# A written order table, loads in smaller pieces, 64x64 transposes, filler matmuls and merged last stores in an attention and channel-mix kernel

## The chip, the cores and the metric

The kernel runs on one core of one Trainium2 chip. The metric is the device time of one execution in microseconds (us). Before the change three runs gave 204.72, 204.80 and 205.69, a median of 204.8.

## What is computed

Inputs are q, k and v, each of 8 batches x 8 heads x 576 positions x 64, two vectors mu_k and mu_r of 512, and three weights: w_k (512x1024), w_v (1024x512) and w_r (512x512). All are float32, and so is the output, 8 x 576 x 512.

```python
q_s = softmax(q over the 64 of a head);  k_s = softmax(k over the 576 positions)
kv  = einsum('bhsd,bhse->bhde', k_s, v);  x = einsum('bhsd,bhde->bhse', q_s, kv)  # heads side by side: 512
x_prev = x one position later, zero at position 0
xk = mu_k*x + (1-mu_k)*x_prev;  xr = mu_r*x + (1-mu_r)*x_prev
k = relu(xk @ w_k);  v = k*k @ w_v;  r = sigmoid(xr @ w_r);  out = r*v
```

The attention has no product of positions by positions: each head makes a 64x64 matrix kv, and q_s is multiplied by it. The channel mix that follows is three dense products over 4608 rows.

## The kernel before

**Attention.** The work goes by (batch b, group g of four heads), 16 pairs in all. A tile holds two heads on its 128 partitions, 64 partitions each with nine positions in a row, and two further heads beside them (index u). The names that the profile shows are these. Loads bring q, k and v as float32 into `raw` buffers, of which there are eleven. Loads of batch 0 (L257) go out on the queues of SP and ACT, those of v of batch 0 (L275) and all later ones on POOL's queue, those of batch 1 in two halves each. ACT takes exponentials of q and k into `eq` and `ek` (L383) and casts v into `vv` (L389). DVE sums q's exponentials, takes reciprocals and scales (L398, L402, L407) into `qs`, all bfloat16.

TensorE (PE) then does three things for the pair. T transposes q: 18 instructions of 64 partitions x 128 columns (L417). KV multiplies exp(k) with v: 36 products of 64x64 (L444), where v has a 65th column of ones that gives the sum Z of exp(k). For batch 0 v has no such column, and 36 more products with a vector of ones make Z (L441). DVE takes 1/Z (`rz`, L451) and scales kv with it (L461); ACT copies the transposed q from PSUM to `qt` (L424). X is the product of the two.

For batches 0 and 1 (`FUSED`) the weights of X already hold mu: DVE multiplies kv with mu and with 1 - mu into `wp` (L538, named wp with batch, group and m), and PE makes xk (m = 0) and xr (m = 1) directly, from q and from q one position earlier (L550); ACT and DVE each copy a half out (L560). For the other batches PE makes x (L591), ACT copies it out, and DVE forms the difference, scales it by mu and adds (L605 to L619). For these the X of one pair, T of the next and KV of the next are one piece of PE work, named B with batch and group in the texts below (TKV where it has no X, and X alone for the last pair). xk and xr stand in SBUF for four batches at a time.

**Channel mix.** 4608 columns are cut into ten units (`UNITS`: 512, 512, 512, 512 and 256 columns, twice). A unit has K, for each of eight 128-row pieces of w_k four matmuls of 128x512 (L687), followed by a relu on ACT (L672) and a square on DVE (L676); then for each tile of 128 rows R, four matmuls with w_r (L719) and a tanh on ACT (L724, which with the +1 in the next step is twice the sigmoid; the relu carries a factor for the half); and V, eight matmuls with w_v (L739), in two halves. DVE multiplies (tanh + 1) with V out of PSUM into one of five `ot` buffers (L745), and two stores of 64 rows of 2 KB each send the tile out (L757). The last tile is worked in two halves of its 512 columns, which gives four stores of 64 rows of 1 KB. Stores go out on SP's queue, the second of each pair of the last tile on ACT's.

**mu.** The two vectors are loaded as two rows (L283). PE spreads them over 128 partitions with one wide matmul and turns them into columns with four small ones (L315, L318); ACT and DVE copy them to SBUF (L324, L328, L330).

**Weights.** w_k comes in two loads of 1 MB (`wk_a`, `wk_b`), w_r in one, w_v in two (`wv_a`, `wv_b`), cast to bfloat16 on the way, on POOL's queue. All loads but the first ones are tied to the sixth load of batch 0 (`GATE`, L338 to L346).

**Order.** No loop over stages sets the order. A list scheduler (`Plan.order`, L158) has a cost for each piece of work, a due time, buffers as resources, and a rule by which PE counts twice when it had little to do lately (`warm`, L124). It picks what can start first and, among equals, what is due first. Each engine then runs its pieces in that order. PSUM has four banks for K, R and V (`mm`) and two pairs of banks for the attention (`att`); for batch 0 and the X of batch 0 either kind is taken (`any`).

Of the kernel before, what the change touches and what calls it, by code (L numbers as in the profile page):

```python
# [26 lines left out]
         "kvn": 2, "wp": 2, "xb": 2, "xd": 2, "xm": 3, "k2": 2, "rel": 3, "th": 2, "ot": 5,  # L27
         "mm": 4, "att": 2, "any": 4}
SHARED = {("any", 0): [("att", 0)], ("any", 1): [("att", 1)],
          ("any", 2): [("mm", 0), ("mm", 1)], ("any", 3): [("mm", 2), ("mm", 3)]}  # L30
KVO = 296
XO = 368

START = 0.7
HOP = 0.05
LATE = 1e6
LOOK = {"PE": 0.03, "ACT": 0.2, "DVE": 0.1, "POOL": 0.03, "SP": 0.03}
MAIN = 5.676
PACE = 1.116
DMA_LEAD = 2.0  # L40
DMA_TAIL = 0.6
LOAD_RATE = 375.0
CAST_RATE = 375.0
GATE = 5
FUSED = (0, 1)
ROWS = 1.05
MU_EARLY = 3.0
BLOCK_LOOK = 0.4
EARLY_UNITS = 2
AHEAD = {(0, 0): 0, (0, 1): 0.64, (1, 0): 3.95, (1, 1): 5.45, (2, 0): 10.46, (2, 1): 5.14, (3,  # L50
        0): 9.42, (3, 1): 7.74, (4, 0): 0, (4, 1): 10.55, (5, 0): 2.05, (5, 1): 11.13, (6, 0):
        16.45, (6, 1): 16.13, (7, 0): 1.76, (7, 1): 3.64}
FIRST = ((0, 0, ("SP", "SP")), (0, 1, ("SP", "SP")), (1, 0, ("SP", "ACT")), (1, 1, ("SP",
        "SP")))
SOON = {(1, 0, 0): 4.53, (1, 0, 1): 4.87}
PASSES = 3


class Slot:

    def __init__(self, pool):
        self.pool = pool
        self.index = None
        self.rank = self.since = None
        self.last = []


class Op:

    def __init__(self, engine, occ, lat, key, emit, deps, takes, gives, size, rate, name):  # L70
        self.engine, self.occ, self.lat, self.key = engine, occ, lat, key
        self.emit, self.deps, self.takes = emit, list(deps), list(takes)
        self.size, self.rate, self.name = size, rate, name
        self.start = self.end = self.made = None
        self.early = 0.0
        self.main = False
        self.look = 0.0
        for slot in gives:
            slot.last.append(self)


class Plan:

    def __init__(self):
        self.pools = {name: [SHARED.get((name, i), [(name, i)]) for i in range(n)]
                      for name, n in POOLS.items()}
        self.ops = []

    def add(self, engine, occ, lat, key, emit, deps=(), takes=(), gives=(), size=0.0, rate=1.0,
            name=""):  # L90
        op = Op(engine, occ, lat, key, emit, [d for d in deps if d is not None], takes, gives,
                size, rate, name)
        self.ops.append(op)
        return op

    def places(self, op):
        t, got = 0.0, []
        for slot in op.takes:
            if slot.index is not None:
                t = max(t, slot.since)  # L100
                continue
            best = None
            if slot.rank is not None and slot.rank != self.next.get(slot.pool, 0):
                return None
            for i, parts in enumerate(self.pools[slot.pool]):
                if (slot.pool, i) in got:
                    continue
                free = 0.0
                for part in parts:
                    user = self.user.get(part)  # L110
                    if user is not None:
                        if not user.last or any(o.end is None for o in user.last):
                            free = None
                            break
                        free = max(free, max(o.end for o in user.last) + HOP)
                if free is not None and (best is None or free < best[0]):
                    best = (free, i)
            if best is None:
                return None
            t = max(t, best[0])  # L120
            got.append((slot.pool, best[1]))
        return t, got

    def warm(self, t):  # L124
        busy = 0.0
        for s, e in reversed(self.pe_busy):
            if e < t - 3.4:
                break
            busy += min(e, t) - max(s, t - 3.4)
        return busy > 2.0  # L130

    def set_due(self):
        for op in self.ops:
            op.due = op.key
        for op in reversed(self.sorted):
            if not op.size and not op.main:
                for o in self.after[op]:
                    op.due = min(op.due, o.due - op.lat - HOP)
                op.due -= op.early

    def prepare(self):
        self.after = {op: [] for op in self.ops}
        for op in self.ops:
            for d in op.deps:
                self.after[d].append(op)
        left = {op: len(op.deps) for op in self.ops}
        ready = [op for op in self.ops if not op.deps]
        self.sorted = []
        while ready:
            op = ready.pop()  # L150
            self.sorted.append(op)
            for o in self.after[op]:
                left[o] -= 1
                if not left[o]:
                    ready.append(o)
        assert len(self.sorted) == len(self.ops)

    def order(self):  # L158
        self.set_due()
        self.user = {}  # L160
        self.next = {}
        self.pe_busy = []
        dma_free = 0.0
        out = {"HW": [], "SW": []}
        free, able, done = {}, {}, []
        left = {}
        for op in self.ops:
            op.start = op.end = None
            for slot in op.takes:
                slot.index = None  # L170
            left[op] = len(op.deps)
            able.setdefault(op.engine, [])
            if not op.deps:
                able[op.engine].append(op)
        n = len(self.ops)
        while len(done) < n:
            chosen = None
            for engine, ops in able.items():
                now = free.get(engine, START)
                ready = None  # L180
                for op in ops:
                    t = now
                    for d in op.deps:
                        t = max(t, d.end + HOP)
                    if op.size:
                        ends = out["SW" if op.engine == "POOL" else "HW"]
                        if len(ends) >= 8:
                            t = max(t, ends[-8] + 0.3)
                    if op.takes:
                        found = self.places(op)  # L190
                        if found is None:
                            continue
                        t = max(t, found[0])
# [8 lines left out]
            for slot, (_, i) in zip(fresh, self.places(op)[1] if fresh else ()):  # L202
                slot.since = t
                slot.index = i
                if slot.rank is not None:
                    self.next[slot.pool] = slot.rank + 1
# [704 lines left out]
```

## Time and profile before

| what | value |
|---|---|
| median of three runs | 204.8 us |
| the profiled execution | 205.87 us, of which the span of the profile is 204.1 |
| PE busy | 187.9 us, 92%, 1930 records |
| weight loads of PE | 93.9 us, 46% (they lie beside matmuls) |
| DVE busy | 152.7 us, 75% |
| ACT busy | 146.8 us, 72% |
| POOL busy | 38.6 us, 19% |
| DMA | 16431 packets, 40.10 MB, mean 197 GB/s |
| the chain that ended last | PE 78%, DMA 13%, DVE 3%, ACT 2% |

The span is what the profiler saw of the program, and the rest of the execution's time lies around it. Busy shares are means over the whole span, so a stage in which one engine waits and a stage in which it never stops are mixed in them; the windows of the prediction take them apart. In a row of a timeline the columns are: start (us), length, engine, line, operation, what is written and what is read, the shape, the count, and in brackets the idle time of the engine just before, with what ended it.

### The profile page before, as it was taken

The page shows a single profiled execution, that of the slowest core. Times are in us where ns is not written, and L with a number is a line of the kernel's source. Part 1 is how long each engine was busy: PE and PEld are TensorE (multiplying, and loading weights), DVE is VectorE, ACT ScalarE, POOL GpSimd, SP SyncE. Part 2 cuts the span into 40 slices and gives each one's busy share as a digit, 9 for nine tenths or more (in the row PEclk, how much of TensorE's full clock was granted, in tenths as well). Part 3 has the DMA queues.
Part 4 walks back from the last instruction along what each step waited for, and adds up shares of the span by engine and source line. Part 5 has one row for each costly group of instructions (what it writes and reads, how often), then busy time and mean ns, then how long its engine had stood idle before and what let it go on. Part 6 is the DMA issues. An engine that isn't in the chain of part 4 may idle for free.

```text
span 204.1 us, 4851 instructions
## 1 busy us (share of the span) xinstructions
PE 187.9 (92%) x1930; PEld 93.9 (46%) x1930; DVE 152.7 (75%) x348; ACT 146.8 (72%) x226; POOL 38.6 (19%) x61
## 2 busy tenths in 40 slices
PE   0659999979999999999999999999999999999990
PEld 0445444534454444444466444444444444444750
DVE  1865478999889989999999995999825459622620
ACT  4463689999999999999999488777624752642520
POOL 4912269433223312532000000000000000000000
PEclk9999999999999999999999999999999999999997
DMA  6999999999999994999742220422044012404303
GB/s 206 277 247 206 256 404 391 399 405 405 392 393 400 410 385 137 368 348 401 224 102 53 48 58 3 100 57 53 0 100 110 0 41 65 103 0 103 90 16 104
DMA packets 16431, 40.10 MB, mean 197 GB/s; under 512 B 2196, under 2 KB 5528, under 8 KB 16408
## 3 DMA queue, kind: packets, MB, share of 16 engines
q0 software_dynamic: 9328, 27.99, 41.6%
q1 hardware_dynamic: 6696, 11.25, 19.7%
q10 hardware_dynamic: 384, 0.56, 0.8%
q8 instruction: 15, 0.25, 0.5%
q14 instruction: 8, 0.07, 0.1%
HBM read 33.56 MB, written 9.44 MB: 211 GB/s over the span
## 4 chain that ended last, share of the span: by engine, by line
PE 78%; DMA 13%; DVE 3%; ACT 2%; POOL 1%; issue 0%; DVEq 0%; ACTq 0%
PE mm_b L739 9%; PE mm_c L739 9%; PE mm_d L739 7%; PE mm_b L687 7%; DMA wr<-in_moe_w_r_dram 7%; PE mm_c L687 7%; PE mm_d L687 7%; PE mm_a L687 7%; PE mm_a L719 6%; DMA raw_g<-in_v_dram 4%; PE mm_a L739 4%; PE mm_d L719 3%; PE mm_c L719 3%; PE mm_b L719 3%; DMA raw_b<-in_q_dram 2%; PE att_b L444 1%
## 5 line engine op out<-in xcount | busy, mean ns | idle before, releaser
L687 PEld LDWEIGHTS <-wk_a 128*128 128x128 bf16 x160 | 15.3, 99 | 17.0 <-issue 1.8
L687 PEld LDWEIGHTS <-wk_b 128*128 128x128 bf16 x160 | 15.5, 98 | 15.3 <-issue 0.2
L719 PEld LDWEIGHTS <-xr 128*128 128x128 bf16 x144 | 13.9, 98 | 16.8 <-ACT xr L563 0.9
L739 PEld LDWEIGHTS <-k_a 128*128 128x128 bf16 x144 | 13.8, 98 | 16.4
L739 PEld LDWEIGHTS <-k_b 128*128 128x128 bf16 x152 | 14.2, 98 | 14.7 <-issue 0.2
L719 PE MATMUL mm_a<-wr,xr 128*128 128x512 bf16 x56 | 14.4, 379 | 0.4 <-DMA raw_g<-in_v_dram 0.4
L724 ACT ACTIVATE th_a<-mm_a 128x512 f32<-128x512 f32 x14 | 8.4, 602 | 7.2 <-PE mm_a L719 7.1
L687 PE MATMUL mm_b<-xk,wk_a 128*128 128x512 bf16 (+1 forms) x44 | 11.2, 371 | 0.0
L687 PE MATMUL mm_c<-xk,wk_a 128*128 128x512 bf16 (+1 forms) x40 | 10.2, 371 | 0.0
L687 PE MATMUL mm_a<-xk,wk_a 128*128 128x512 bf16 (+1 forms) x40 | 9.8, 360 | 0.3 <-DVE xk L560 0.3
L687 PE MATMUL mm_c<-xk,wk_b 128*128 128x512 bf16 (+1 forms) x40 | 9.4, 358 | 0.0
L687 PE MATMUL mm_d<-xk,wk_b 128*128 128x512 bf16 (+1 forms) x40 | 9.4, 358 | 0.0
L687 PE MATMUL mm_a<-xk,wk_b 128*128 128x512 bf16 (+1 forms) x40 | 9.4, 358 | 0.0
L687 PE MATMUL mm_b<-xk,wk_b 128*128 128x512 bf16 (+1 forms) x40 | 9.4, 358 | 0.0
L687 PE MATMUL mm_d<-xk,wk_a 128*128 128x512 bf16 (+1 forms) x36 | 9.2, 368 | 0.0
L315 PE MATMUL mm_a<-mu_rows,pick 2*128 2x512 f32 x2 | 2.0, 1122 | 6.8 <-DMA mu_rows<-in_moe_mu_r_dram 6.8
L719 PE MATMUL mm_d<-wr,xr 128*128 128x512 bf16 x32 | 8.2, 379 | 0.0
L719 PE MATMUL mm_b<-wr,xr 128*128 128x512 bf16 x28 | 7.2, 379 | 0.0
L719 PE MATMUL mm_c<-wr,xr 128*128 128x512 bf16 x28 | 7.2, 379 | 0.0
L676 DVE TENSOR_TENSOR k_a<-rel_a 128x512 bf16<-128x512 bf16 (+1 forms) x13 | 5.1, 391 | 2.8 <-ACT rel_a L672 2.6
L672 ACT ACTIVATE rel_b<-mm_a 128x512 bf16<-128x512 f32 (+1 forms) x7 | 4.0, 571 | 4.1 <-PE mm_a L687 3.9
L676 DVE TENSOR_TENSOR k_a<-rel_c 128x512 bf16<-128x512 bf16 (+1 forms) x13 | 5.1, 392 | 2.4 <-ACT rel_c L672 2.3
(323 smaller groups left out, 487.7 us busy)
## 6 DMA issues: line engine op xcount, KB each, us to landing
out_dram<-ot_a SPq DMA_DIRECT2D x14, 128.0 KB, 2.4
out_dram<-ot_b SPq DMA_DIRECT2D x14, 128.0 KB, 2.4
out_dram<-ot_c SPq DMA_DIRECT2D x14, 128.0 KB, 3.2
out_dram<-ot_d SPq DMA_DIRECT2D x14, 128.0 KB, 2.7
raw_k<-in_v_dram POOLq DMA_DIRECT2D x3, 576.0 KB, 8.5
out_dram<-ot_e SPq DMA_DIRECT2D x13, 128.0 KB, 2.4
raw_j<-in_k_dram POOLq DMA_DIRECT2D x2, 576.0 KB, 10.7
raw_a<-in_q_dram POOLq DMA_DIRECT2D x2, 576.0 KB, 10.1
```

Of the source, the lines that this page charges most:

```text
L315: nc.tensor.matmul(kn.bank(wide_slot), lhsT=kn.pick[:].rearrange("p u c -> p (u c)"), rhs=kn.mu_rows[:].rearrange("p m c -> p (m c)"), sta ...
L444: kn.nc.tensor.matmul(to, lhsT=by, rhs=kn.vvs[vv.index][two[r], j, u, 0:65], **flags)
L672: kn.nc.scalar.activation(out=kn.rels[rel.index][:, 0:n], in_=kn.bank(kf)[:, 0:n], func=ACT.Relu, scale=HALF_ROOT)
L676: kn.nc.vector.tensor_tensor(out=kn.k2s[k2.index][:, fc, 0:n], in0=kn.rels[rel.index][:, 0:n], in1=kn.rels[rel.index][:, 0:n], op=ALU.mult)
L687: kn.nc.tensor.matmul(kn.bank(kf)[:, 0:n], lhsT=kn.wk[fc // 4][:, ct, (fc % 4) * 128:(fc % 4) * 128 + 128], rhs=kn.xs[0][:, ct, c0:c0 + n] ...
L719: kn.nc.tensor.matmul(kn.bank(rps), lhsT=kn.xs[1][:, ct, c:c + 128], rhs=kn.wr[:, ct, :], start=(ct == 0), stop=(ct == CT - 1))
L724: kn.nc.scalar.activation(out=kn.ths[th.index][:], in_=kn.bank(rps), func=ACT.Tanh, scale=0.5)
L739: kn.nc.tensor.matmul(kn.bank(vps)[:, 0:width], lhsT=kn.k2s[k2.index][:, ft, 128 * m:128 * m + 128], rhs=kn.wv[ft // 4][:, ft % 4, part], ...
```

## The change

The scheduler with its costs and due times is gone. In its place stands a table, `ORDER`, with one entry for each piece of work, carried out in that order; an entry names the piece, where needed the engine (`ACT!`), and the buffers of the pools it takes. What is in the table and around it:

- **Loads.** w_k comes in four pieces of half a MB (half of its columns, and every second of its four row blocks), w_v in three (row blocks 0-3, 4-5 and 6-7, of 1, 0.5 and 0.5 MB). There is no tie to the sixth load any more. On POOL's queue the halves of batch 1's q stand between the pieces of w_k, and the last two pieces of w_v behind the last of batch 1. Of batch 0 one half of q and two halves of k go out on ACT's queue instead of SP's, and so does the load of mu's rows.
- **Transposes.** For ten of the 16 pairs (all but those in `WHOLE`) T is 36 transposes of 64x64 in the place of 18 of 64x128.
- **X alone.** The X of pair (2,1) stands alone as that of the last pair did (`ALONE`), and so B of pair (3,0) becomes TKV30.
- **Batch 0.** KV is split by u, with Z as a piece of its own of 18 products of 64x128 for the pair, 36 over the two pairs in place of 72.
- **Filler matmuls.** 22 matmuls of zeros, 128x512 (L292), stand between the first pieces of PE. Their results are not read.
- **mu.** The columns come from a load of their own on POOL's queue and one transpose on PE (L272), late; the wide matmul stays early.
- **wp.** For batch 1 the weights for xr (wp101 and wp111, two multiplications each) are made by POOL, not DVE.
- **Stores.** The product with V is written over the tanh in place: seven `th` buffers stand for the two `th` and five `ot`. Each store of 64 rows is an entry of its own. The last unit's two tiles are stored differently: the first tile by one store of 128 rows, the last by two of 128 half rows, whose output address has the two groups of 64 as outermost count (`[C, 2], [J * C, 64], [1, width]`).

The table, its first lines and its last:

```
ACT!rows ident load00q0:0 load01q1:1 ACT!load00q1 load01q0 load00v consts load00k0:2 load01v zero
load01k1:3 fill:3 warm load10q1:4 fill.2:2 fill.3:3 wk00 fill.4:2 fill.5:3 expq000:0 load10q0
fill.6:2 ACT!load00k1 rsum000:0 wk10 wide:0 ACT!load01k0 expq011:1 load11q1:5 expq010 rsum011:1
wk01 fill.7:3 rrec000 expq001 rsum010 fill.8:2 fill.9:3 rrec010 rrec011 rsum001 fill.10:2
...
relu97:2 sq96 sq97 r91:1 th90:2 v900:2 th91:1 v910:0 v901 v911 o90 v910.2:3 o91 st90 v911.2 st91
o91.2 st91.2
```

And the core of the diff:

```diff
-    "kvn": 2, "wp": 2, "xb": 2, "xd": 2, "xm": 3, "k2": 2, "rel": 3, "th": 2, "ot": 5,
+    "kvn": 2, "wp": 2, "xb": 2, "xd": 2, "xm": 3, "k2": 2, "rel": 3, "th": 7,
...
+FILLS = 45
+WHOLE = ((0, 0), (0, 1), (1, 0), (1, 1), (2, 0), (3, 0))
+ALONE = ((2, 1), (B - 1, 1))
...
+    def ordered(self):
+        ops = {op.name: op for op in self.ops}
+        for token in ORDER.split():
+            name, _, places = token.partition(":")
+            engine, _, name = name.rpartition("!")
+            op = ops[name]
...
+            for slot, place in zip(fresh, places.split(".")):
+                slot.index = int(place)
...
+            yield op
...
-        for i in range(4):
-            nc.tensor.matmul(
-                kn.bank(mu_slot)[:, 2 * i:2 * i + 2],
-                lhsT=kn.mu_rows[:].rearrange("p m c -> p (m c)")[:, 128 * i:128 * i + 128],
-                rhs=kn.pick[:, :, 0], start=True, stop=True)
...
+    def emit_mu():
+        kn.nc.tensor.transpose(out=kn.bank(mu_slot)[:, 0:8], in_=kn.mu_sb[:],
+                               identity=kn.identf[:])
...
+        def fill(slot=slot):
+            kn.nc.tensor.matmul(kn.bank(slot), lhsT=kn.still[:, 0:128],
+                                rhs=kn.still[:], start=True, stop=True)
...
-                for r in range(2):
-                    kn.nc.tensor.transpose(out=turned(slot, r)[:, 64 * j:64 * j + 64],
-                                           in_=kn.qss[qs.index][two[r], j, :],
-                                           identity=kn.ident[two[r], two[r]])
+                for u in ((slice(0, 128),) if (b, g) in WHOLE else two):
+                    for r in range(2):
+                        kn.nc.tensor.transpose(
+                            out=turned(slot, r)[u, 64 * j:64 * j + 64],
+                            in_=kn.qss[qs.index][two[r], j, u],
+                            identity=kn.ident[two[r], two[r]])
...
-                            kn.nc.tensor.matmul(kn.half(qtp, r)[two[u], KVO + 64:KVO + 65],
-                                                lhsT=by, rhs=kn.one[two[r], :], **flags)
+                    kn.nc.tensor.matmul(kn.half(slot, r)[:, KVO + 64:KVO + 65],
+                                        lhsT=kn.eks[ek.index][two[r], j].rearrange(
+                                            "p u d -> p (u d)"),
+                                        rhs=kn.one[two[r], :], start=(j == 0),
+                                        stop=(j == J - 1))
...
-    wk_done = [add("POOL", 0.75, 0.75, h, lambda h=h: weight(
-        kn.wk[h], kn.w_k, F, 512 * h, 512, h == 0), gate, size=1048.0, rate=CAST_RATE,
-        name=f"wk{h}") for h in range(2)]
+    wk_done = [[add("POOL", lambda h=h, g=g: weight(kn.wk[h][g], kn.w_k, F, g, 2, 2, 512 * h),
+                    name=f"wk{h}{g}") for g in range(2)] for h in range(2)]
...
-                wdone = add("DVE", 0.4, 0.48, step, lambda m=m: mixed_weights(m),
-                            [ndone, wide_done], [wp], [kvn], name=f"wp{tag}{m}")
+                wdone = add("POOL" if m and b else "DVE", lambda m=m: mixed_weights(m),
+                            [ndone, wide_done], [wp], [kvn], name=f"wp{tag}{m}")
...
-                        out=kn.ots[ot.index][:, part], in0=kn.ths[th.index][:, part],
+                        out=kn.ths[th.index][:, part], in0=kn.ths[th.index][:, part],
...
-                    for i in range(2):
-                        jb = (RING * half + c) // 64 + i
-                        bb, j = jb // J, jb % J
-                        dst = bass.AP(tensor=kn.out.tensor,
-                                      offset=kn.out.offset + (bb * S + j) * C + part.start,
-                                      ap=[[J * C, 64], [1, width]])
-                        q = kn.nc.scalar if len(parts) == 2 and i == 1 else kn.nc.sync
-                        q.dma_start(out=dst, in_=kn.ots[ot.index][64 * i:64 * i + 64, part])
+                    jb = (RING * half + c) // 64 + i
+                    bb, j = jb // J, jb % J
+                    dst = bass.AP(tensor=kn.out.tensor,
+                                  offset=kn.out.offset + (bb * S + j) * C + part.start,
+                                  ap=[[C, k], [J * C, 64], [1, width]])
+                    kn.queues[queue].dma_start(
+                        out=dst, in_=kn.ths[th.index][64 * i:64 * (i + k), part])
...
+                end = last and m >= tiles - 2
+                for i in range(1 if end else 2):
+                    queue = "ACT" if end and len(parts) == 2 and not part.start else "SP"
+                    add(queue, lambda i=i, k=2 if end else 1, q=queue, f=store: f(i, k, q), [o],
+                        [], [th], name=f"st{index}{m}")
```

## The prediction

> **What bounds the kernel now.** I read the windows of four stages first, cut where TensorE (PE) starts unit 1, where it starts unit 4, and at its last matmul. Columns: stretch, length, then busy us (and instructions) of PE, weight loads, DVE, ACT and POOL, clock, DMA share, GB/s.
>
> ```profile
> 0.00:43.78 43.78, 32.90 (x474) 17.98 (x475) 29.54 (x85) 30.16 (x50) 21.18 (x37) 1.00 1.06 305
> 43.78:103.75 59.97, 59.97 (x695) 28.40 (x692) 57.55 (x114) 59.37 (x83) 17.38 (x24) 1.00 0.94 347
> 103.75:198.82 95.07, 95.07 (x767) 47.54 (x765) 65.16 (x150) 57.25 (x96) 0.00 (x0) 1.00 0.24 57
> 198.82:204.07 5.25, 0.00 (x0) 0.00 (x0) 0.42 (x1) 0.00 (x0) 0.00 (x0) 0.79 0.34 101
> ```
>
> A is a ramp: PE is busy 32.9 of 43.8, DMA all of it. In B PE never stops, and ACT (59.37 of 59.97) has no room either. C is PE alone. D is the last stores and the end of the program. The execution took 205.87, so E = 205.87 - 204.07 = 1.8 lies outside the span; the three plain runs have a median of 204.8, 1.1 lower.
>
> Next the timeline of PE, for the ramp.
>
> ```profile
> 17.57 1.03 PE L687 MATMUL mm_a<-xk,wk_a 128*128 128x512 bf16 x2
> 18.39 1.06 PE L687 MATMUL mm_b<-xk,wk_a 128*128 128x512 bf16 x2
> ...
> 22.55 0.59 PE L687 MATMUL mm_b<-xk,wk_a 128*128 128x512 bf16 x2
> 22.98 0.59 PE L687 MATMUL mm_c<-xk,wk_a 128*128 128x512 bf16 x2
> ...
> 43.16 0.44 PE L550 MATMUL att_a<-qt_b,wp_a 64*64 64x288 bf16 x8 [1.15 <-ACT xk L560]
> 43.78 0.60 PE L687 MATMUL mm_a<-xk,wk_a 128*128 128x512 bf16 x2
> ```
>
> Two matmuls of 512 columns step by 0.82 at 17.6 and by 0.43 at 22.5: the array ran at half speed until about 21 (the column that says 1.00 doesn't show it). One such matmul is 0.41 slow, 0.216 fast.
>
> What PE waits for there is loading. In POOL's timeline each issue waits for the landing of the eighth before it, so it dates the landings:
>
> ```profile
> 15.35 0.54 POOL L257 DMA_DIRECT2D raw_f<-in_k_dram  x1 [2.66 <-DMA wk_a<-in_moe_w_k_dram]
> ...
> 26.18 0.54 POOL L257 DMA_DIRECT2D raw_h<-in_q_dram  x1 [2.12 <-DMA wv_b<-in_moe_w_v_dram]
> ...
> 28.40 0.54 POOL L257 DMA_DIRECT2D raw_j<-in_v_dram  x1 [0.21 <-issue]
> 29.16 0.54 POOL L257 DMA_DIRECT2D raw_j<-in_v_dram  x1 [0.21 <-issue]
> ```
>
> wk_a to wv_b is four weights of 1 MB in 10.8: 2.7 each. Half loads follow at 0.75.
>
> Last the end: the page's queue and issue lines, then the DMA view of 198 to 204.1, whose GB/s are 40 slices of 0.15.
>
> ```profile
> q1 hardware_dynamic: 6696, 11.25, 19.7%
> raw_j<-in_v_dram POOLq DMA_DIRECT2D x2, 288.0 KB, 5.7
> out_dram<-ot_a ACTq DMA_DIRECT2D x2, 64.0 KB, 3.2
> ```
>
> ```profile
> GB/s 0 0 0 0 0 0 0 0 0 107 269 201 201 229 376 370 329 115 161 275 329 148 202 108 13 27 20 13 0 0 0 0 0 0 0 0 0 0 0 0
> DMA packets 481, 0.53 MB, mean 87 GB/s; under 512 B 96, under 2 KB 352, under 8 KB 480
> ```
>
> raw_j lands 5.7 after 29.16: batch 1 is complete at 34.9. The six last stores move 0.53 MB from 199.4 to 202.2, with 96 small packets: 16 completions each.
>
> **The change part by part.**
>
> Loads (A). Up to 34.9 the same bytes move, reordered: pieces of wk alternate with batch 1's q, the second half of wv comes last. Backwards from 34.9: wv's last quarter 34.9, the one before 33.6, batch 1's last k half 32.2, first half of wv 32.2 - 6 x 0.75 = 27.7, wr 23.5 (2.7 and two half loads earlier), wk 20.0 and 18.7. The gate on the weights goes; bandwidth then sets the same total. Moving mu's rows to ACT and two k halves behind ACT's first exponential costs nothing: ten 0.75 loads of batch 0 share the bandwidth until 12 to 13 either way.
>
> PE in A. K of unit 0 (32 x 0.216 = 6.9) and R (3.5) fit between wk and wr and end near 28; V's first halves (16 x 0.216 = 3.5) follow wv to 31.2, TKV10 0.9. TKV11 waits for the k half at 32.2 and its exponential (0.7): 32.9 to 33.8. Three quarters of V (0.43 each) reach 35.1, then five more and two X (0.62): 3.4. Unit 1 starts at 38.5 instead of 43.8. Low 37.5, if nothing after 27.7 waits (27.7 + 6.9 + 1.7 + 1.2); high 43.8, if before's waits return. A new wait: mu's transpose stands on PE just before X110, and X110 and unit 1 queue behind it; its load lies behind one that lands at 36.4, a margin of about 1.
>
> Zero matmuls: 15 before the first transposes, 15 x 0.41 + 2.0 for the mu product from about 2 ends at 10.2; before's transposes began at 10.3 and still wait for DVE's four scalings. Seven more lie in waits before wk at 18.7. Cost 0; without that cover 7 x 0.41 = 2.9. Half the Z products, wp on POOL (four of DVE's 0.28, behind load issues that wait for landings; X111 and X101 need them, some 3 later) and the mu work on PE all lie beside waits: 0.
>
> Blocks. X, T, KV start at 60.45, 60.82, 61.19 and end at 61.60. X's 512 columns need 0.216 of the 0.32 after 60.50, so about 0.1 is a change of tile shape; T's 18 become 36 like KV's 36 in 0.41, without its exit. Per block -0.17 (from +0.05, KV's full price and no change saved, to -0.2). In C five blocks: 95.1 - 0.8 = 94.3 (93.9 to 95.4). In B ACT forbids it, and hides the 0.1 of X21 standing alone: the same ACT instructions stand between the same points. Batch 2 follows 34.9 at 1.5 a load (q 37.9, 39.4, 40.9, k 42.4) and ACT takes it in order before copies that unit 1 needs, for which I add 1: B = 61.0 (59.4 to 63). Output buffers (seven th for two th and five ot) and single-half stores add no SP issue: 0.
>
> The end. Before, four stores closed the last tile and two the one ahead; now one store writes 128 rows and two write 128 half rows, each with its output address as 2 x 64 rows, outermost 2. Which engines carry it? The count on SP's queue tells: 7 loads of 128 rows + 16 completions and 71 stores of 64 + 16 are 6688 packets; the 8 left are the two loads of mu, 2 rows and 2 completions each. So a transfer whose outermost count is 2 went over 2 engines, where all others went over 16. That one had only 2 rows in all; whether 2 x 64 rows also stay on 2 no row shows. [...] By rows alone: two engines move 0.52 MB at 373/16 = 23.3 GB/s each (the best slices above) in 11.2; at the page's 405 in 10.4; at the 187 mean of an isolated pair of stores (167.4 to 168.8), 22 (total 220). I take 11.2, the nearest row, from the same stores. First byte 0.6 after the last matmul (199.4), last byte to end 1.8 (202.2 to 204.07): D = 13.6. Over 16: last issue 0.5 after the matmul, landing 2.5, end 1.2: 4.2.
>
> Sum: 38.5 + 61.0 + 94.3 + 13.6 + 1.8 = 209.2. The profiled execution's 1.1 over the median is not taken off, since the ramp that may hold it is replaced.
>
> **The rivals.**
> Faster: the three stores spread over 16 engines by their 128 rows. D = 4.2, total 199.8. It decides when D is under about 9. For: SBUF's side is 128 rows; against: the two completions.
> Ramp not gained: ACT, not loading, paces unit 1, as its 1.15 at 43.16 suggests; A = 43.8, total 214.5, or 205.1 with spread stores. Against: batch 1 lands 2.7 earlier and its q far earlier.
> The change doesn't do what it says: program reads (the packets of kind "instruction") now stop PE; B blocks have 36 rows more. Against: no wait in B or C was for issue. Up to 2 on the forecast.
>
> **How the numbers follow.** Two engines with the ramp gained 0.55, spread stores with the ramp gained 0.30, no ramp gain 0.08 and 0.07. The forecast is 209.2; its own range, with A to 41, B to 63 and D from 12.8 to 17, is 206 to 214. A tail at 22 stays outside, under 0.05. The whole range goes down to 198, which holds most of the faster rival (199.8 -1.8): 198 to 214 leaves out under 0.2. About 0.5% (1.0) is what a measurement here can tell. Slower: 0.53 + 0.08 = 0.61; same: 0.02 + 0.03 = 0.05; faster: 0.30 + 0.04 = 0.34.
>
> **What would show it.** Unit 1's first matmul near 38.5; clock fast before 18; ACT still over 98% in B; X, T and KV together under 1.05; and over 10 us of slices near 47 GB/s after the last matmul, with 2 completions for each of the three stores. I am wrong if that tail is under 5, or if PE waits in B for ACT by more than 3.

## The result and the profile after

The changed kernel takes 211.5 us (210.96 to 212.09) against 205.2 of the kernel before (204.72 to 205.69): 1.031 times as long, with a 95% interval of 1.026 to 1.035. Executions over 1.5% slower than the fastest of their kernel count in the median times below and are left out of the ratios. The profiled execution took 212.09, its span is 210.3. The ramp became shorter, as forecast, though by half as much; the two middle stretches changed little; the end became 9 longer.

The windows of the changed kernel, cut at the same four points: unit 1's first matmul, unit 4's first matmul, the last matmul, the end. Columns: stretch, length, then busy us (and instructions) of PE, weight loads, DVE, ACT and POOL, clock, DMA share, GB/s.

```profile
0.00:41.06 41.06, 37.70 (x453) 16.97 (x453) 27.38 (x81) 29.61 (x48) 24.49 (x44) 0.96 1.06 302
41.06:101.28 60.22, 59.78 (x784) 28.33 (x781) 58.52 (x117) 58.79 (x82) 19.00 (x27) 1.00 0.96 358
101.28:195.97 94.69, 94.53 (x857) 47.69 (x855) 65.27 (x150) 57.56 (x96) 0.00 (x0) 1.00 0.26 60
195.97:210.28 14.31, 0.00 (x0) 0.00 (x0) 0.42 (x1) 0.00 (x0) 0.00 (x0) 0.68 0.11 37
```

Against the forecast, with E the time outside the span:

| stretch | before | forecast | after |
|---|---|---|---|
| A, to unit 1 | 43.78 | 38.5 | 41.06 |
| B, to unit 4 | 59.97 | 61.0 | 60.22 |
| C, to the last matmul | 95.07 | 94.3 | 94.69 |
| D, the end | 5.25 | 13.6 | 14.31 |
| E | 1.8 | 1.8 | 1.8 |
| profiled execution | 205.87 | 209.2 | 212.09 |

D first. The DMA view of the stretch after the last matmul, whose GB/s are 40 slices of 0.36:

```profile
GB/s 0 6 23 17 11 34 34 17 40 46 40 51 51 43 51 51 51 51 49 51 51 51 46 51 49 46 51 46 49 49 46 51 46 51 46 14 0 0 0 0
DMA packets 390, 0.52 MB, mean 37 GB/s; under 512 B 6, under 2 KB 262, under 8 KB 390
q1 hardware_dynamic: 260, 0.39, 8.4%
q10 hardware_dynamic: 130, 0.13, 2.6%
```

The rate is flat at about 50 GB/s for 8 us, about an eighth of the best slices of before (370 to 376), and PE has nothing to do. There are 256 + 128 rows in the three stores, so 6 of the 390 packets, those under 512 B, are no rows: two for each store, called completions here. Before there were 16 for each. SP's queue alone (q1) moved 40 to 51 GB/s before the first packet of ACT's (q10) at 200.5, and both together stay at 50. By the DMA view the packets of SP's queue took 12.4% of the time of 16 engines from 196.7 to 200.5, those of both queues 13.4% from 200.5 to 208.5: the time of 2.0 and of 2.1 engines. That both queues use the same two is an estimate from these shares; no view names the engines.

Next PE's timeline in the ramp, at unit 0's first K, its first V, batch 1's transposes and unit 1:

```profile
18.75 0.65 PE L601 MATMUL mm_a<-xk,wk_aa 128*128 128x512 bf16 x2 [0.16 <-DVE xk L492]
...
30.75 1.03 PE L653 MATMUL mm_a<-wv_a,k_a 128*128 128x512 bf16 x4
...
35.08 0.44 PE L361 MATMUL att_a<-ident,qs_a 64*128 64x64 bf16 x18
...
41.06 0.60 PE L601 MATMUL mm_d<-xk,wk_aa 128*128 128x512 bf16 x2
```

Between 18.75 and 41.06 no row has a wait in brackets but the first. PE is busy 22.3 of 22.3 there, so nothing that lands in this time sets its end.

A block, X, T and KV, from the timelines of the changed kernel and then of the kernel before:

```profile
68.54 0.22 PE L517 MATMUL att_b<-qt_c,w_c 64*64 64x64 bf16 x4
68.59 0.39 PE L517 MATMUL att_a<-qt_c,w_c 64*64 64x512 bf16 x4
68.81 0.48 PE L361 MATMUL att_b<-ident,qs_b 64*64 64x64 bf16 x36
69.11 0.57 PE L391 MATMUL att_b<-vv_c,ek_b 64*64 64x65 bf16 x36
```

```profile
70.34 0.22 PE L591 MATMUL att_b<-qt_c,w_c 64*64 64x64 bf16 x4
70.39 0.39 PE L591 MATMUL att_a<-qt_c,w_c 64*64 64x512 bf16 x4
70.71 0.44 PE L417 MATMUL att_b<-ident,qs_b 64*128 64x64 bf16 x18
71.08 0.48 PE L444 MATMUL att_b<-vv_c,ek_b 64*64 64x65 bf16 x36
```

From X to T it is 0.27 in place of 0.37, from T to KV 0.30 in place of 0.37. The whole block, up to the next matmul, takes 1.07 in place of 1.15, as the KV of this one is 0.08 longer; most blocks take 0.99.

And one wait that the kernel before does not have, in ACT's waits between unit 1 and unit 4 (columns: who waited for whom, us in total, times, longest):

```profile
ACT th_b L638 <- DMA out_dram<-th_b: 1.1, 1, 1.1
```

The tanh of unit 2's second tile is written into a buffer whose old content a store is still sending.

### The profile page after: what moved, and what is told of

It reads as the page before. It is cut to its first block, busy times and chain, and to the rows that moved or that the text cites. A ratio compares the mean times of both kernels' runs of the same rounds, so it can differ in the third digit from the quotient of the medians.

```text
span 210.3 us, 5189 instructions
## 1 busy us (share of the span) xinstructions
PE 192.0 (91%) x2089; PEld 93.0 (44%) x2089; DVE 151.6 (72%) x347; ACT 146.0 (69%) x224; POOL 43.5 (21%) x70
## 4 chain that ended last, share of the span: by engine, by line
PE 79%; DMA 9%; DVE 3%; SPq 1%; ACT 1%; issue 1%; DVEq 0%; ACTq 0%
PE mm_a L653 9%; PE mm_c L653 8%; PE mm_c L601 7%; PE mm_b L653 7%; PE mm_a L601 7%; PE mm_d L601 6%; PE mm_b L601 6%; PE mm_d L633 6%; DMA out_dram<-th_e 4%; PE mm_d L653 4%; PE mm_b L633 4%; DMA raw_c<-in_k_dram 4%; PE mm_a L633 2%; PE mm_c L633 2%; DMA raw_a<-in_q_dram 1%; PE att_b L391 1%
## 5 line engine op out<-in xcount | busy, mean ns | idle before, releaser
L653 PEld LDWEIGHTS <-k_b 128*128 128x128 bf16 x152 | 14.3, 98 | 15.0 <-issue 0.5
L633 PE MATMUL mm_d<-wr,xr 128*128 128x512 bf16 x52 | 13.4, 379 | 0.1
L601 PEld LDWEIGHTS <-wk_ab 128*128 128x128 bf16 x80 | 7.7, 98 | 8.2 <-DVE xk L489 0.5
L601 PEld LDWEIGHTS <-wk_bb 128*128 128x128 bf16 x80 | 7.8, 98 | 7.8
L601 PEld LDWEIGHTS <-wk_ba 128*128 128x128 bf16 x80 | 7.6, 98 | 7.9 <-issue 1.1
L601 PEld LDWEIGHTS <-wk_aa 128*128 128x128 bf16 x80 | 7.4, 98 | 8.4 <-issue 1.3
L292 PE MATMUL mm_d<-still 128*128 128x512 bf16 x13 | 7.2, 557 | 1.9 <-DVE still L233 1.9
L633 PE MATMUL mm_a<-wr,xr 128*128 128x512 bf16 x28 | 7.2, 379 | 0.0
L592 DVE TENSOR_TENSOR k_b<-rel_c 128x512 bf16<-128x512 bf16 (+1 forms) x15 | 5.8, 389 | 1.5 <-ACT rel_c L588 0.9
L601 PE MATMUL mm_c<-xk,wk_ba 128*128 128x512 bf16 (+1 forms) x22 | 6.1, 360 | 0.5 <-ACT th_b L638 0.3
L523 ACT CAST xb_a<-att_a 128x1024 bf16<-128x1024 f32 x5 | 5.3, 1064 | 1.4 <-PE att_a L517 1.4
L653 PE MATMUL mm_c<-wv_a,k_b 128*128 128x512 bf16 x24 | 6.2, 379 | 0.0
```

The lines of the kernel that those rows point to most:

```text
L292: kn.nc.tensor.matmul(kn.bank(slot), lhsT=kn.still[:, 0:128], rhs=kn.still[:], start=True, stop=True)
L523: kn.nc.scalar.copy(out=kn.xbs[xb.index][:, :, 64:576], in_=kn.whole(pair))
L592: kn.nc.vector.tensor_tensor(out=kn.k2s[k2.index][:, fc, 0:n], in0=kn.rels[rel.index][:, 0:n], in1=kn.rels[rel.index][:, 0:n], op=ALU.mult)
L601: kn.nc.tensor.matmul(kn.bank(kf)[:, 0:n], lhsT=kn.wk[fc // 4][ct % 2][:, ct // 2, (fc % 4) * 128: (fc % 4) * 128 + 128], rhs=kn.xs[0][:, ...
L633: kn.nc.tensor.matmul(kn.bank(rps), lhsT=kn.xs[1][:, ct, c:c + 128], rhs=kn.wr[:, ct, :], start=(ct == 0), stop=(ct == CT - 1))
L653: kn.nc.tensor.matmul(kn.bank(vps)[:, 0:width], lhsT=kn.k2s[k2.index][:, ft, 128 * m:128 * m + 128], rhs=wv_of(ft)[:, part], start=(ft == ...
```

## The experiments

The time of each run is a median; the ratio is to the kernel before, with its 95% interval. "First K" is unit 0's first K, and A to D are the stretches of each profile, read from PE's timeline.

| kernel | time | ratio | first K | A | B | C | D |
|---|---|---|---|---|---|---|---|
| split_last | 203.8 | 0.983 [0.973, 0.992] | 18.9 | 42.0 | 61.4 | 94.6 | 4.6 |
| before_merged | 215.2 | 1.047 [1.042, 1.051] | 18.1 | 44.3 | 60.0 | 95.1 | 14.7 |
| outer4 | 209.3 | 1.017 [1.013, 1.022] | 17.8 | 40.5 | 61.7 | 94.6 | 10.2 |
| no_fills | 202.6 | 0.986 [0.982, 0.990] | 17.7 | 40.4 | 60.5 | 94.6 | 4.6 |
| st10_early | 202.1 | 0.981 [0.976, 0.986] | 19.9 | 42.7 | 59.4 | 94.6 | 4.6 |
| r_quarter | 200.6 | 0.972 [0.967, 0.977] | 16.9 | 38.8 | 59.3 | 94.4 | 4.6 |
| t_whole | 203.7 | 0.987 [0.981, 0.992] | 20.7 | 43.3 | 60.2 | 95.1 | 4.6 |
| wv_first | 202.0 | 0.981 [0.979, 0.984] | 19.8 | 42.0 | 59.3 | 94.4 | 4.6 |
| best | 200.8 | 0.977 [0.974, 0.980] | 17.7 | 39.9 | 59.3 | 94.4 | 4.6 |
| fills_early | 199.8 | 0.973 [0.970, 0.977] | 16.1 | 38.8 | 59.3 | 94.4 | 4.6 |
| fills_late | 202.9 | 0.986 [0.983, 0.989] | 20.8 | 43.0 | 59.3 | 94.4 | 4.6 |
| gated_nofill | 201.4 | 0.979 [0.976, 0.983] | 18.5 | 42.1 | 59.3 | 94.4 | 4.6 |

The first K comes anywhere from 16.1 to 20.8, so of the ramp a single profile tells less than of the rest. Executions of split_last lay between 200.6 and 206.9. From the first K to unit 1 it is 22.2 to 23.6 in every version of the changed kernel that keeps the whole R, however early or late the first K comes: unit 1 follows the first K.

**The last stores.** Three kernels tell the address from the rest of the change.

```diff
 split_last, against the changed kernel
-                for i in range(1 if end else 2):
-                    queue = "ACT" if end and len(parts) == 2 and not part.start else "SP"
-                    add(queue, lambda i=i, k=2 if end else 1, q=queue, f=store: f(i, k, q), [o],
+                for i in range(2):
+                    queue = "ACT" if end and len(parts) == 2 and i else "SP"
+                    add(queue, lambda i=i, k=1, q=queue, f=store: f(i, k, q), [o],
```

> The changed kernel with only its last three stores taken back to six of 64 rows each (four of 1 KB rows, on both queues, for the last tile). Theory: the tail of 14.3 after the last matmul comes from the three stores running on two DMA engines. Then the tail falls to 4.2 to 5.3 and the profiled execution from 212.1 to about 202.5; against the kernel before -1.0 to -2.0%. Rival: the tail is the price of 128 rows or of fewer queues' work at the end whatever the address form, or the earlier stages were themselves disturbed by it; then the tail stays over 8 and the time over 206. The stages ahead of the last matmul should stay at 41.1, 60.2 and 94.7 by either.

```diff
 before_merged, against the kernel before, in store()
-                    for i in range(2):
+                    end = last and m >= tiles - 2
+                    for i in range(1 if end else 2):
+                        k = 2 if end else 1
...
-                                      ap=[[J * C, 64], [1, width]])
+                                      ap=[[C, k], [J * C, 64], [1, width]])
```

> The kernel before with only the last stores changed, to the three that the change has. Theory: two DMA engines carry them, 2 completions each, and the tail goes from 5.3 to about 14.3: 214 in the profiled execution, +4.4% against the kernel before. Rival: the tail belongs to something else in the change (th written in place, the order at the end); then the time stays within 1 of before.

```diff
 outer4, against split_last
-                                  ap=[[C, k], [J * C, 64], [1, width]])
+                                  ap=([[J * C, 4], [4 * J * C, 16], [1, width]]
+                                      if last and m >= tiles - 2 else [[J * C, 64], [1, width]]))
```

> As split_last, but each of the six last stores has an output address of 4 x 16 rows instead of 64 (every fourth row first; the rows of the last two tiles land in another order, the bytes are the same). Theory: the outermost count sets how many DMA engines carry a store. Then each store has 4 completions, the six run at about twice the 48 GB/s of the changed kernel's tail, 0.52 MB take 5.6, and the tail is about 8 (time about 3 over split_last). Rival: only a count below some number of rows is special, or the number of stores matters and not the address; then tail and time are those of split_last within 1.

The DMA views of their ends: before_merged, then outer4 (slices of 0.26), then split_last (slices of 0.15).

```profile
DMA packets 391, 0.53 MB, mean 36 GB/s; under 512 B 6, under 2 KB 262, under 8 KB 390
```

```profile
GB/s 0 0 16 48 32 8 32 32 96 32 80 40 96 100 92 56 56 72 56 80 80 96 76 84 92 96 92 96 96 80 60 28 24 24 0 0 0 0 0 0
DMA packets 408, 0.52 MB, mean 51 GB/s; under 512 B 24, under 2 KB 280, under 8 KB 408
```

```profile
GB/s 0 0 0 0 0 0 0 0 0 0 137 246 218 205 178 362 335 218 205 130 184 239 328 82 150 219 62 0 0 0 0 0 0 0 0 0 0 0 0 0
DMA packets 480, 0.52 MB, mean 87 GB/s; under 512 B 96, under 2 KB 352, under 8 KB 480
```

Six small packets for three stores, 24 for six, 96 for six: 2, 4 and 16 completions a store, as the outermost count of the address goes from 2 to 4 to 64, and the best slices go from 51 in the changed kernel (55 in before_merged) to 100 to 362 GB/s. In the kernel before, one store of the last unit's first tile goes out on ACT's queue as well (at 198.3), and in before_merged that tile's only store does, where the change has it on SP's; the flat rate is the same. Merged stores alone lengthen the kernel before by 9.5 in D, and split stores take 9.7 out of the changed one. The tail of outer4 was forecast at 8 and measures 10.2, since its slices reach 100 only at times and not throughout: the transfer takes 8.0 for the 5.6 expected. The time of the packets goes with the counts. The two queues together took 11.0% of the time of 16 engines in the changed kernel's view, 18.1% in outer4's and 33.0% in split_last's, in windows of 14.31, 10.23 and 6.00; over transfers of 12.0, 8.0 and 2.6 that is the time of 2.1, 3.7 and 12 engines. Which engines carry a store, and why, no view shows.

**The store that the tanh waits for.** Written in place, the product frees its buffer only when its store has landed. In the table st10, the two stores of unit 1's first tile, stands on SP's queue behind a store of a later tile: its product is done at 62.1 in split_last, and it leaves at 66.8.

```diff
 st10_early, against split_last (the order table)
-X21:0.1 mix201 v101 th20:3 load50q0:7 rrec310 sc2001 xb21:1 v110:2 mix200 xs21 o10 v130:3
+X21:0.1 mix201 v101 th20:3 load50q0:7 rrec310 sc2001 xb21:1 v110:2 mix200 xs21 o10 st10 st10.2 v130:3
...
-st12.2 rz30:0 sc2111 k23:3 relu27:1 st10.2 w30:2 scale310:1 relu22:2 st10 load51v0:2 k21:1 qt30:2
+st12.2 rz30:0 sc2111 k23:3 relu27:1 w30:2 scale310:1 relu22:2 load51v0:2 k21:1 qt30:2
```

> split_last with one order changed: the two stores of unit 1's first tile stand on SP's queue right behind the product that they send, ahead of a store of a later tile. Seen so far: between unit 1 and unit 4 (60.2, 61.4, 61.7 in three runs of the change's order) ACT waits 1.1 to 2.4 for the landing of that store, since the next tanh is written into the same buffer (the change writes the product over the tanh), and PE then waits 0.3 to 1.7 for the tanh. Theory: this one wait is what the stretch has lost; it goes, and the stretch takes 59.3 to 59.8. Rival: the wait moves to the next store or to a load, as ACT has no room there anyway; the stretch stays at 60.2 or more.

The waits of ACT and of PE in split_last, in the stretch B:

```profile
ACT th_b L638 <- DMA out_dram<-th_b: 2.3, 1, 2.3
```

```profile
PE mm_c L601 <- ACT th_b L638: 1.6, 1, 1.6
```

In st10_early the tanh's wait and PE's for it are gone, PE is busy throughout, and B is 59.4 (59.3 in the later runs of that order with 64x64 transposes) in place of 60.2 to 61.7. So a single place in the order cost 0.8 to 2.3.

**Transposes.**

```diff
 t_whole, against st10_early
-WHOLE = ((0, 0), (0, 1), (1, 0), (1, 1), (2, 0), (3, 0))
+WHOLE = tuple((b, g) for b in range(B) for g in range(2))
```

> st10_early with all transposes of 64x128. Theory: a block of X, T and KV costs 1.15 again in place of 0.99 (0.374, 0.366, 0.410 against 0.272, 0.297, 0.419), so the stretch from unit 4 to the last matmul, with five such blocks, takes 0.8 longer: 95.4; in the stretch before it, where ACT is full, less than half of the same shows. Rival: only T itself changes, 0.07 a block, and X's first 0.1 belongs to something else; then the last stretch is 94.9.

B and C of st10_early, then of t_whole:

```profile
42.67:102.09 59.42, 59.42 (x784) 28.27 (x781) 58.45 (x117) 58.97 (x82) 18.35 (x26) 1.00 0.97 355
102.09:196.69 94.60, 94.52 (x857) 47.67 (x855) 65.35 (x150) 57.49 (x96) 0.00 (x0) 1.00 0.26 60
```

```profile
43.32:103.50 60.18, 60.18 (x694) 28.25 (x691) 58.78 (x117) 59.45 (x82) 17.47 (x25) 1.00 0.95 349
103.50:198.57 95.07, 95.07 (x767) 47.49 (x765) 65.36 (x150) 57.26 (x96) 0.00 (x0) 1.00 0.25 58
```

C is 0.5 longer with whole transposes, or 0.7 against the 94.4 of the other runs of that order: less than the 0.8 of the rows, more than the rival's 0.3. Four of the five blocks differ by 0.16 and one by 0.05 (1.10 and 1.15), which together is the 0.7. X's 0.1 does come back (0.374 in t_whole), so the rival falls. B is 0.76 longer, nearly all of five blocks at 0.16, where less than half was expected. ACT has 0.45 to 0.73 free there and does not hide it.

**PE's own work in the ramp.** r_quarter leaves out three quarters of unit 0's R, so its tanh is of a part of the sum.

```diff
 r_quarter, against st10_early
-                for ct in range(CT):
+                cts = range(CT if index else 1)
+                for ct in cts:
...
-                                        stop=(ct == CT - 1))
+                                        stop=(ct == cts[-1]))
```

> st10_early with unit 0's R cut from four matmuls a tile to one (12 matmuls left out, 2.6 of PE at 0.216, in the stretch from unit 0's first K to unit 1's; the tanh of unit 0 is then of a part of its sum). Theory: PE's own work fills the ramp from unit 0's first K on (22.3 of 22.3 busy in the change's profile), which the forecast of 38.5 had laid against landings instead; then unit 1 starts 2.0 to 2.6 earlier counted from unit 0's first K: 19.7 to 20.6 in place of 22.3 to 23.1. Rival: landings of batch 1 (last half of k at 32.1) or ACT pace it, and PE only waits longer; then the stretch stays within 1 of 22.3.

```diff
 wv_first, against st10_early (the order table; the two are taken out further on)
-X001:3.1 x0000 x0001 load10k0 expq100:2 edge01 k02:0 x0011 x0010 k03:1 wv0 rsum100:2 X010:0.1
+X001:3.1 x0000 x0001 load10k0 expq100:2 edge01 k02:0 x0011 x0010 k03:1 wv0 wv1 wv2 rsum100:2 X010:0.1
```

> st10_early with the last two pieces of w_v loaded right behind the first, ahead of batch 1's last halves, as the kernel before had them. Theory: batch 1's last half of k lands 2.4 later (34.5 in place of 32.1), PE waits for it at its T and KV of batch 1 in a fixed order, and unit 1 starts 1 to 2 later. Rival: as PE is busy from unit 0's first K on, the order of these loads costs nothing; unit 1 starts within 0.5.

From the first K to unit 1 it is 22.2 to 22.8 in wv_first, st10_early, t_whole and best, and 21.9 in r_quarter: of 2.6 taken away only 0.3 to 0.9 came out. The theory failed as it was put. The timeline of r_quarter at batch 1's T and KV tells why; below it is the same place in fills_early.

```profile
31.72 0.44 PE L361 MATMUL att_b<-ident,qs_c 64*128 64x64 bf16 x18
32.09 0.48 PE L391 MATMUL att_b<-vv_a,ek_c 64*64 64x65 bf16 x36
32.98 0.44 PE L361 MATMUL att_a<-ident,qs_a 64*128 64x64 bf16 x18 [0.41 <-DVE qs_a L350]
```

```profile
32.97 0.44 PE L360 MATMUL att_a<-ident,qs_a 64*128 64x64 bf16 x18
33.34 0.48 PE L390 MATMUL att_a<-vv_b,ek_a 64*64 64x65 bf16 x36
33.75 0.60 PE L652 MATMUL mm_c<-wv_b,k_a 128*128 128x512 bf16 x2
```

r_quarter began early, at 16.9, and came to batch 1 at 31.7, before it was ready: PE waits 0.4 for DVE's last scaling of q, besides 0.7 for a relu ahead of it. ACT's exponential of batch 1's last half of k, landed at 32.2, ends at 33.0 as well. Both kernels begin TKV11 at 33.0 and unit 1 at 38.80, which is the earliest start of any run, but not for the same reason. fills_early has the whole R and its first K at 16.1; it comes to TKV11 without a wait, DVE's scaling having ended at 32.7, after one wait of 0.5 for ACT's copy of xk early on.

So there are two limits. With the whole R, PE's 22.3 of work counted from the first K decides (22.2 to 23.6 in all). With less of it the readiness of batch 1 comes into play: by its work alone r_quarter would start unit 1 at 16.9 + 22.3 - 2.6 = 36.6, and it starts at 38.8. The marked waits are 1.1 of these 2.2; the rest is in short gaps, such as steps of 0.5 for one matmul of R, whose cause stays open. wv_first had its first K at 19.8, PE waited only 0.2 for xk at that K, and the order of the loads cost nothing. It was close: batch 1's last half of k landed at 35.8, later than expected, and its exponential ended at 36.5, just when PE began the KV that reads it. With a first K at 16 that order may cost.

**The fillers.**

```diff
 no_fills against split_last; best, fills_early (the first 15 kept) and
 fills_late (the last seven kept) against st10_early
-load01k1:3 fill:3 warm load10q1:4 fill.2:2 fill.3:3 wk00 fill.4:2 fill.5:3 expq000:0 load10q0
+load01k1:3 warm load10q1:4 wk00 expq000:0 load10q0
```

> split_last without the 22 filler matmuls. Theory: they keep the array at full speed when unit 0's first K comes at 18.75; without them it runs at half speed until about 21.5, as in the kernel before, and unit 1 starts 1.3 to 2 later than 41.1; time +0.6 to +1.0% against split_last. Rival one: PE catches up, because loads or ACT pace the ramp; no difference within 0.5. Rival two: the fillers stand in the way of T00, Z and X000, which then come up to 1 earlier, and the ramp ends as early or earlier.

> st10_early without the 22 filler matmuls: stores split, the late store early, no fillers. In no_fills the granted clock was 1.00 throughout and the time from the first transpose to X000 4.0; in four of the seven profiles with fillers the clock fell to 0.50 to 0.80 between 10 and 20, and that time was 5.9 to 7.3. Theory: the fillers bring the low clock and cost 1 to 2 on average; without them unit 1 starts at 40.0 to 40.8, the stretch to unit 4 takes 59.4, the next 94.5, the tail 4.6: 200 to 201 in the profiled execution, -2.1 to -2.7% against the kernel before. Rival: the low clock belongs to the chip and the moment, not to the fillers; then it shows here too, and the time is that of st10_early (202).

> st10_early with only the 15 fillers ahead of the first transposes. Theory one: eight us of unbroken 512-column matmuls ahead of the real work bring the low clock; then it shows here (below 0.9 somewhere between 10 and 20) in about half of the runs and the time is near 202. Theory two: the seven fillers inside batch 0's chain bring it, or cost by standing in front of work that is ready; then the clock stays at 1.00 and the time is that of best.

> st10_early with only the seven fillers that stand between batch 0's pieces. Theory one: without the early ones no low clock, and the late ones cost at most their own length where work is ready (7 x 0.22 to 0.42 is 1.5 to 2.9, most of it beside waits): within 1 of best. Theory two: as in fills_early, these bring the low clock or the delay; then the first transpose to X000 takes 5 to 7 and the time is near 202.

The expectations took the clock column for the sign of a slow array. The durations show that it is not enough. PE's timeline of fills_late, fillers between batch 0's pieces, and of fills_early, none there:

```profile
14.23 0.61 PE L290 MATMUL mm_d<-still 128*128 128x512 bf16 x1
14.78 0.40 PE L376 MATMUL att_b<-one,ek_a 64*128 64x1 bf16 x18
15.11 0.61 PE L290 MATMUL mm_d<-still 128*128 128x512 bf16 x1
15.51 0.63 PE L290 MATMUL mm_c<-still 128*128 128x512 bf16 x1
```

```profile
11.31 0.66 PE L390 MATMUL att_b<-vb_a,ek_a 64*64 64x64 bf16 x36
11.90 0.38 PE L377 MATMUL att_b<-one,ek_a 64*128 64x1 bf16 x18
```

In fills_late a filler is 0.61 to 0.63 with steps of 0.40 and more: half speed, though the clock column says 1.00 from 10 to 26. At full speed the row says 0.38. The profiles with all 22 fillers fall in two kinds. In outer4 and r_quarter the array stays fast and the first transposes to X000 take 4.4 and 4.8. In the five others a pair of fillers inside batch 0's chain takes 0.83 to 0.96, which is half speed, and the same stretch takes 5.9 to 7.3. In four of these the array had been fast before and has fallen back; in split_last it was not yet fast, as the rows of T (0.66) and KV (0.99) ahead of the pair show. With no filler (no_fills, best, gated_nofill) it takes 3.8 to 4.0, at half speed all the way; with the early ones alone 3.3, T, KV and Z at full speed. So the late seven stand in front of work that is ready, and at half speed they cost 3.3 (7.1 in fills_late for 3.8 in best). fills_late at 0.986 [0.983, 0.989] is slower than best and fills_early beyond their intervals; between those two, 0.977 [0.974, 0.980] and 0.973 [0.970, 0.977], nothing is settled. For K the fillers do count: in all nine profiles with fillers its first two matmuls step by 0.22 to 0.28, which is near full speed, and in four of the five without any by 0.39 to 0.40. In best the first four matmuls of K take 1.01 from 17.70 on, in gated_nofill 1.71 from 18.50 on.

In no_fills rival two comes nearest (X000 1.9 earlier than in split_last, unit 1 1.6 earlier, the time not told apart). best came out as its theory had it, 199.95 in the profile, though its interval and that of st10_early overlap. In fills_early and fills_late theory two holds: the late seven are the ones that cost.

**The gate.**

```diff
 gated_nofill, against best (the order table)
-load01k1:3 warm load10q1:4 wk00 expq000:0 load10q0
+load01k1:3 warm load10q1^load01q1:4 wk00 expq000:0 load10q0
```

> best with POOL's first load of batch 1 held until the fourth first load of batch 0 (01q1) has landed, about 4.3, as the kernel before held its weights (its first weight load left at 4.87; in the change POOL's loads start at 3.0). In the change the halves of q of batch 0 that go second land at 5.1 and 7.4 where the kernel before had both of the first group's by 5.3, and the first transposes start at 11.5 to 12.3 in place of 10.3. Theory: the early loads of POOL take bandwidth from batch 0 and cost the first transposes about 1; held, T00 starts near 10.8, X000 and unit 0's first K 0.7 earlier, and unit 1 too, as PE is busy from then on. Rival: the weights come as much later and PE waits for wk or for batch 1 in place of T00; unit 1 starts no earlier.

POOL's first load left at 5.03 in place of 3.00, and the first transposes came at 12.7, later than the 12.1 of best; unit 1 came at 42.1 for 39.9. The theory's gain does not show, as the rival had it: nothing here points to the missing gate as what made T00 later than the 10.3 of the kernel before. It is one profile, and T00 lies between 10.8 and 12.4 in the others of the change, so a small effect is not ruled out. The halves of q that land late in the profiles of the change (5.1 to 8.4 for a half that had landed by 5.3 before) go out on ACT's queue behind mu's rows; that this is the cause was not tried.

**The version to keep.** fills_early (split stores, st10 early, 15 fillers) takes 199.8 against 205.4 before: 0.973, the shortest of all kernels that do the whole computation, though not told apart from best. Its four stretches are 38.8, 59.3, 94.4 and 4.6.

## Why the prediction was right, and where it was not

**The end: right, in rate and in length.** The time of 2.1 engines, 2 completions a store, a flat 46 to 51 GB/s: D was forecast at 13.6 and is 14.31. That 2 x 64 rows stay on two engines no run had shown before the result, as the 2 completions were those of two loads of 2 rows; the changed kernel and before_merged then showed 2 for each of the three stores. The term that was a little small is the transfer, 12.0 from first to last packet (196.68 to 208.66) for 11.2. before_merged and split_last show that these three stores, and nothing else of the change, make the kernel slower than before. The faster rival, spread stores, is split_last: 199.8 was forecast for it, and its profiled execution took 204.3: the ramp is 3.5 longer than forecast, B, C and D 0.3 to 0.4 each.

**The ramp: right in direction, wrong in its limit.** Of the 2.9 by which the profiled execution exceeds the forecast, the ramp has 2.6. The landings came as worked out: wr 23.8 (23.5), first half of wv 27.7 (27.7), last k half 32.1 (32.2), last piece of wv 34.5 (34.9). The step that failed is "end near 28" for K and R. Counted from its own first K, at 18.75, PE has K 6.9, R 3.5, V 6.9, four X 2.5, two TKV 1.6 and mu 0.2, in all 21.6 with no wait, and measures 22.3. So K, R and the X between them end at 30.75, and unit 1 starts at 41.06. The forecast put each piece against a landing and did not add up PE's pieces: from its own 18.7 for the last of wk's first half, K and R alone come to 29.1, and the two X that stand between them (1.2) have no term. Its 38.5 lies near the other limit, the readiness of batch 1, at which r_quarter starts unit 1 at 38.80; in the changed kernel PE does not wait for it.

**"Cost 0" for the fillers: wrong.** They were laid beside waits. The first 15 do lie there; the seven in batch 0's chain do not, and the chain's end, not wk at 18.7, starts unit 0. That K would find a fast array was right (18.75, steps of 0.22 to 0.27), and the fillers have a part in it, as four of the five profiles without them show half speed there. "Moving mu's rows to ACT ... costs nothing" stays doubtful: T00 starts at 11.5 for 10.3, and holding POOL's first load did not bring that back.

**Blocks: right.** 0.162 a block measured in most, 0.17 forecast. In C five blocks brought 0.4 of 0.8 in the changed kernel, and 0.7 in most kernels after it. (The low end of C, 93.9, is a slip: five times -0.2 gives 94.1.)

**B: right in sum by two errors.** "In B ACT forbids it" is wrong: t_whole shows 0.76 of the blocks' 0.81 there. "Output buffers ... add no SP issue: 0" counted issues and missed that a tanh now waits for a store's landing, 1.1 in ACT and 0.3 in PE in the change's own profile, up to 2.4 and 1.7 in others. The 1 added for batch 2's place on ACT did not show: without that wait B is 59.3, less than before. Of "program reads" no wait of PE showed in the changed kernel's B or C.

## What to carry to other kernels

Count the completions of a store before merging it with another: the outermost count of its address decided over 2 or 16 completions here, 50 or 360 GB/s in the best slices, and at the end of this program nothing hid it (14.3 for 4.6). Before a stage is called bound by loading, add up what the busiest engine has to do in it from its first real instruction on; the later of the two sums is the forecast. Where a buffer is reused in place, the next writer waits for the store (a tanh for 2.3 in split_last), so a store's place on its queue can come onto the critical path; and filler work belongs only where the engine surely waits.

## What was not expected of the hardware

The column of the granted clock and the array's speed differ. In fills_late, best and the kernel before it says 1.00 where the rows show half speed: fillers that step by 0.40 and more in fills_late, where two of fills_early's at full speed step by 0.21; a KV of 0.99 in best, for 0.66 in fills_early; two matmuls of K in 0.82 at 17.6 in the kernel before, in 0.43 at 22.5. In the changed kernel and three others with all fillers it falls to 0.50 to 0.69 in a window of 4 us between 10 and 18, where the rows show that same half speed (in the changed kernel a filler of 0.61 at 15.17, for 0.38 at 17.11). In split_last, too, it says 1.00 at half speed (fillers of 0.61 and 0.63). In all these profiles the half speed that the column leaves out comes before the array has first been fast, and the half speed that it shows comes after. So the speed is to be read from the step between equal matmuls. The same instructions in the same order gave a fast array in two profiles and a half-speed one in five. What decides between the two no run here shows.
